# Ten dense matmuls of the mixing tables ahead of the first strided unit of batch 0

## The chip, the cores and the metric

The kernel runs on one core of one Trainium2 chip. The metric is device time in microseconds (us) of one execution, as the median of several runs. TensorE (PE) multiplies, VectorE (DVE) and ScalarE (ACT) work on rows of data, GpSimd (POOL) and SyncE (SP) here mostly issue DMA transfers. Each engine takes its instructions in one fixed order.

## The reference, cut to what matters

Inputs are q, k, v of 4 batches, 8 heads, 576 tokens and head size 64, then two mixing networks with weights of 512 x 2048 and 2048 x 512 each.

```
mask_local   = (rel >= 0) & (rel < 32)                       # heads 0 to 3
mask_strided = (rel >= 0) & (pos[None, :] % 32 == pos[:, None] % 32)   # heads 4 to 7
attn = softmax(where(mask, q @ k.T / 8, -1e9));  x = attn @ v          # per batch and head
x = x laid out as (batch, 576, 512)
h = x.transpose(0, 2, 1) @ U @ V;  u = x + h.transpose(0, 2, 1)
x = u + relu(u @ w_ch1) @ w_ch2                              # first network
u = x + real(fft2(x));  un = layer_norm(u)
out = u + relu(un @ w2_ch1) @ w2_ch2                         # second network
```

## The kernel before, in words

The attention of a batch is cut into nine units, taken in the order `L00, L10, L01, L11, R, S00, S10, S01, S11`: four local ones, one for the rest rows, and four strided ones (`strided_unit`), S*ji* for head pair *j* and half *i* of the token groups. A strided unit has three steps. First the mask is written into a PSUM bank by one matmul (L472) and the scores are added to it by five or six matmuls (L477). The maximum of each row is taken (L412) and negated (L415) on DVE, and ACT makes six exponentials (L420). Then three transposes on PE (L484) and two copies on ACT (L494, L491). Last the product with v, six matmuls (L500), and on DVE a reciprocal and a multiply (L425, L426, L432 in `norm_out`) that leave the unit's result in the tile `xs`. Banks of PSUM come from `bank()` in a fixed rotation.

When the four strided units of a batch are done, `unpermute` writes `xs` to DRAM (L554, L555 on SP's queue) and reads it back in the order of the tokens (L559, L561). Meanwhile `mix_groups` multiplies the rows with the table `US` (L577), and `VS` turns that back into 512 columns (L617), which L618 adds to the rows that `unpermute` has brought. `US` and `VS` are the mixing tables U and V, spread over 128 rows at the start; both are in the format f32r. Then `prep_tile` scales and splits the rows (L660, L143 to L147, L155, L158), transposes them on PE (L647), and the first layer of network 1 begins (L978 to L980), then its second (L1005 to L1007).

Beside this the lane of the weights runs: 512 KB pieces come by DMA into three buffers (`raw`, L162) and are turned from f64 bits into f32 (L135 to L139), squared for their scale (L213) and split in two f16 parts (L155, L158), on the same ACT and DVE. `wnow[0]` holds from the start until the second row tile of network 1 is prepared: batch 0's attention lies within it.

The code is written out as lanes that are stepped in a fixed sequence, and a scheduler then settles for each engine, when the kernel is built, in which order its instructions stand. A change in one place can so change the order of other instructions around it.

Of the kernel before, what the change touches and what calls it, by code (L numbers as in the profile page):

```python
# [35 lines left out]
RWIN = [256, 289]  # L36
MAGIC = 0x5F3759DF
RAWS = 3
BSEQ = [0, 1, 0, 1, 2]
PB = 1  # L40
LOADS = ['l0', 'm', 'v1', 'r', 'v0', 'l1', 'w', 's0', 'w', 'x0', 'w', 's1', 'x1']
# [30 lines left out]
def fused_kernel(ctx: ExitStack, tc: tile.TileContext, ql, kl, vl, vr, qs, ks, vs, uraw, vraw,  # L72
                 w11, w12, w21, w22, cb, cf, ft, out):
    nc = tc.nc
    V, A, T, G, S = nc.vector, nc.scalar, nc.tensor, nc.gpsimd, nc.sync

    const = ctx.enter_context(tc.tile_pool(name="const", bufs=1))
    wp = ctx.enter_context(tc.tile_pool(name="wp", bufs=1))
    rawp = ctx.enter_context(tc.tile_pool(name="rawp", bufs=RAWS))
    tmp = ctx.enter_context(tc.tile_pool(name="tmp", bufs=2))  # L80
# [8 lines left out]
    wnow = [True]  # L89

    def bank():
        if wnow[0]:
            nbk[0] += 1
            z = BSEQ[nbk[0] % len(BSEQ)]
            if z:
                return (pf1, pf2)[z - 1].tile([128, 512], F32, tag=f"f{z}", name="bk")
        return pb.tile([128, 512], F32, tag="b", name="bk")
# [69 lines left out]
    def fetch():  # L167
        if todo:
            src, m = todo.pop(0)
            pre.append((src, m, wload(src, m)))  # L170
# [106 lines left out]
    US = cst.tile([128, 12, 128], F32R, name="US")  # L277
    VS = cst.tile([128, 960], F32R, name="VS")
# [22 lines left out]
    def p_buf():  # L301
        if wnow[0]:
            return early_buf("gh", 416)
        return atp.tile([128, 416], F32, tag="P", bufs=PB, name="P")
# [103 lines left out]
    def softmax_rows(P, Sb, r, groups):  # L408
        mx = atp.tile([128, 8], F32, tag="mx", bufs=3, name="mx")
        c = 0  # L410
        for o, n, w in groups:
            V.tensor_reduce(out=mx[r, c:c + n], in_=Sb[r, o:o + n * w].rearrange("p (n w) -> p n w", n=n),  # L412
                            axis=AX.X, op=ALU.max)
            c += n
        V.tensor_scalar(out=mx[r, 0:c], in0=mx[r, 0:c], scalar1=-0.125, scalar2=None, op0=ALU.mult)  # L415
        c = 0
        for o, n, w in groups:
            for i in range(n):
                a = o + i * w
                A.activation(out=P[r, a:a + w], in_=Sb[r, a:a + w], func=AF.Exp,  # L420
                             scale=0.125, bias=mx[r, c:c + 1])
                c += 1
# [5 lines left out]
    def norm_out(O, dst, r, n):  # L428
        Ov = O[r, 0:130 * n].rearrange("p (n h w) -> p n h w", h=2, w=65)
        rc = atp.tile([128, 3, 2, 1], F32, tag="rc", bufs=3, name="rc")  # L430
        recip(rc[r, 0:n], Ov[:, :, :, 64:65])
        V.tensor_tensor(out=dst.rearrange("p n (h w) -> p n h w", h=2), in0=Ov[:, :, :, 0:64],  # L432
                        in1=rc[r, 0:n].to_broadcast([r.stop - r.start, n, 2, 64]), op=ALU.mult)
# [34 lines left out]

    def strided_unit(b, j, u, q, k, v, xs):
        Sb = bank()  # L470
        msk = mS[u].rearrange("p (n w) -> p n w", n=1).to_broadcast([128, 3, 128]) if u else mS[u]
        T.matmul(Sb[:, 0:384], lhsT=idb, rhs=msk, start=True, stop=True)  # L472
        for i in range(6):
            g = 6 * u + i - (u or i > 0)
            if u == 0 and i == 1:
                continue
            T.matmul(Sb[SROW, 64 * i:64 * i + 54], lhsT=q[:, 108 * g:108 * g + 108], rhs=k[:, 54 * g:54 * g + 54],  # L477
                     start=False, stop=True, skip_group_check=True)
        P = p_buf()
        softmax_rows(P, Sb, SROW, [(0, 6, 64)])  # L480
        yield
        Tb = bank()
        for t in range(3):
            T.transpose(Tb[:, 108 * t:108 * t + 108], P[SROW, 128 * t:128 * t + 128], ident[SROW, SROW])  # L484
        npz[0] += 1
        PT = early["pz"] if wnow[0] and npz[0] % 2 else PZ
        for e in range(2):
            r = slice(64 * e, 64 * e + 64)
            src = Tb[r, 0:324].rearrange("p (n c) -> p n c", c=54)
            if e:  # L490
                A.activation(out=PT[r, :, 27:81], in_=src, func=AF.Copy)  # L491
            else:
                dst = PT[r].rearrange("p n (f c) -> p n f c", c=27)[:, :, 0:4:3, :]
                A.activation(out=dst, in_=src.rearrange("p n (f c) -> p n f c", c=27), func=AF.Copy)  # L494
        yield
        O = bank()
        for t in range(3):
            for h in range(2):
                c = 65 * (2 * t + h)
                T.matmul(O[SROW, c:c + 65], lhsT=PT[:, 2 * t + h, :], rhs=v[:, 3 * u + t, h, :],  # L500
                         start=True, stop=True, skip_group_check=True)
        norm_out(O, xs[SROW, 3 * u:3 * u + 3, 128 * j:128 * j + 128], SROW, 3)
        yield
# [29 lines left out]
    def attn_units(b):  # L533
        xs = atp.tile([128, NT, 256], F32, tag="xs", bufs=1, name="xs")
        qk_upto(4 * b + 3)
        v = loaded if b == 0 else {n: VT[n[0]](b, int(n[1:] or 0)) for n in ("v0", "v1", "r", "x0", "x1")}
        for u in ORDER:
            if u == "R":
                yield u, rest_unit(b, qk[4 * b:4 * b + 2], v["r"]), xs
                qk_upto(4 * b + (5 if b else 4))  # L540
                continue
            j, i = int(u[1]), int(u[2])
            if u[0] == "L":
                yield u, local_unit(b, j, i, *qk[4 * b + j], v[f"v{j}"]), xs
            else:
                yield u, strided_unit(b, j, i, *qk[4 * b + 2 + j], v[f"x{j}"], xs), xs
                if i == 1 and b:
                    qk_upto(4 * b + 6 + j)
# [478 lines left out]
    def weights():  # L1027
# [6 lines left out]
        todo.extend((w, i) for w in (w21, w22) for i in range(NW))  # L1034
        for _ in range(RAWS):
            fetch()
# [279 lines left out]
```

## Time and the profile before

| | us |
|---|---|
| median of 3 runs | 967.18 (966.31 to 968.62) |
| profiled execution, its own time | 960.7 |
| its span, first to last instruction | 958.9 |
| PE busy | 910.7 (95% of the span) |
| DVE busy | 595.8 (62%) |
| ACT busy | 393.3 (41%) |
| mean granted clock of PE | 0.98 of full speed |

The profile tells of one execution. Its own time is 1.8 us more than its span and 6.5 us less than the median of the three runs; times in the rows are counted from the start of the span. Full speed of PE's clock is 2.4 GHz and its other level 1.2 GHz, shown as 1.00 and 0.50.

### The profile page before, as it was taken

Reading aid. Unit: us, or ns where it says so; the run is one execution under the profiler, and the core shown is the slowest. Engines: PE = TensorE matmul, PEld = TensorE weight load, DVE = VectorE, ACT = ScalarE, POOL = GpSimd, SP = SyncE. Lnnn points to the kernel's source line nnn. Section 1 sums busy time; section 2 is a strip of 40 time slices with the busy share of each in tenths; the row PEclk is TensorE's granted clock in tenths of the full one; section 3 lists DMA queues with packets and bytes.
Section 4 is the critical chain, followed back from the end, with each engine's and each line's share of the span. In section 5 each row is a group of like instructions: output and inputs, shape, how many; then the busy total and the mean of one; then the engine's idle time right before and its main releaser. Section 6 shows DMA issues by size and latency. Waiting matters only on the chain. (4 is left out here: it accounts for less than half of the span.)

```text
span 958.9 us, 14895 instructions
## 1 busy us (share of the span) xinstructions
PE 910.7 (95%) x5696; PEld 541.8 (57%) x5696; DVE 595.8 (62%) x1526; ACT 393.3 (41%) x947; POOL 48.9 (5%) x81
## 2 busy tenths in 40 slices
PE   5858999999999999999999989999999999999998
PEld 4737754555545664466456436555544657576565
DVE  3788888833342446862879998982799853142323
ACT  4867677624141434631447454241333333032122
POOL 0111011000000001100101300010000000000000
PEclk9859999999999999999999989999999999999999
DMA  9576675232211103601334520002022310200000
GB/s 298 166 260 196 204 263 163 67 117 96 65 23 23 39 3 118 155 22 34 100 94 127 127 72 1 1 19 70 1 55 50 94 23 1 61 2 1 23 23 23
DMA packets 68791, 78.58 MB, mean 82 GB/s; under 512 B 46384, under 2 KB 51760, under 8 KB 68720
## 3 DMA queue, kind: packets, MB, share of 16 engines
q1 hardware_dynamic: 59696, 44.49, 16.7%
q0 software_dynamic: 9024, 33.14, 10.9%
q8 instruction: 45, 0.74, 0.3%
q14 instruction: 26, 0.21, 0.1%
HBM read 60.18 MB, written 7.08 MB: 70 GB/s over the span
## 5 line engine op out<-in xcount | busy, mean ns | idle before, releaser
L1005 PE MATMUL f<-wslot,gh 128*128 128x512 f16 x576 | 218.1, 379 | 2.3 <-DVE ub L1013 1.9
L1006 PE MATMUL f<-wslot,gh 128*128 128x512 f16 x576 | 218.1, 379 | 0.1
L1007 PE MATMUL f<-wslot,gl 128*128 128x512 f16 x576 | 218.1, 379 | 0.0
L978 PE MATMUL f<-ut,wslot 128*128 128x512 f16 (+1 forms) x480 | 170.3, 355 | 9.9 <-DVE gl L985 9.2
L979 PE MATMUL f<-ut,wslot 128*128 128x512 f16 (+1 forms) x480 | 169.8, 354 | 1.1 <-DMA ut<-lo 1.1
L980 PE MATMUL f<-ut,wslot 128*128 128x512 f16 (+1 forms) x480 | 169.6, 353 | 0.0
L1013 DVE SCALAR_TENSOR_TENSOR ub<-f,ivt,ub 128x512 f32<-128x512 f32 x64 | 47.7, 746 | 113.2 <-PE f L1007 113.0
L984 ACT ACTIVATE gh<-f 128x512 f16<-128x512 f32 (+1 forms) x120 | 64.0, 535 | 120.2 <-PE f L980 119.7
L985 DVE SCALAR_TENSOR_TENSOR gl<-f,gh 128x512 f16<-128x512 f32 (+1 forms) x120 | 73.8, 615 | 55.1 <-ACT gh L984 54.3
L1007 PEld LDWEIGHTS <-gl 128*128 128x128 f16 x576 | 56.4, 98 | 66.9 <-issue 0.3
L1006 PEld LDWEIGHTS <-gh 128*128 128x128 f16 x576 | 56.7, 98 | 63.9 <-issue 2.8
L1005 PEld LDWEIGHTS <-gh 128*128 128x128 f16 x576 | 57.0, 99 | 63.0 <-issue 0.2
L979 PEld LDWEIGHTS <-wslot 128*128 128x128 f16 x480 | 47.4, 99 | 52.7 <-issue 15.4
L978 PEld LDWEIGHTS <-wslot 128*128 128x128 f16 x480 | 47.6, 99 | 43.8 <-issue 4.7
L980 PEld LDWEIGHTS <-wslot 128*128 128x128 f16 x480 | 47.3, 99 | 43.2 <-issue 1.6
L155 ACT ACTIVATE wslot<-wslot,wsc 128x512 f16<-128x512 f32 x64 | 46.0, 719 | 32.5 <-DVE wslot L158 22.2
L135 ACT ACTIVATE wslot<-raw 128x512 f32<-128x512 f32 x64 | 42.8, 675 | 38.5 <-DMA raw<-in_w 27.5
L906 ACT ACTIVATE wslot<-X 128x512 f32<-128x512 f32 (+1 forms) x24 | 12.6, 524 | 101.6 <-PE X L901 101.6
L158 DVE SCALAR_TENSOR_TENSOR wslot<-wslot,wsc 128x512 f16<-128x512 f32 x64 | 48.6, 759 | 5.4 <-ACT wslot L155 5.3
L162 POOL DMA_DIRECT2D raw<-in_w x61 | 33.4, 547 | 310.0 <-DVE fa L707 61.8
L213 ACT ACTIVATE wslot<-wslot 128x512 bf16<-128x512 f32 x64 | 40.3, 630 | 18.8 <-DVE wslot L139 16.3
L420 ACT ACTIVATE P<-bk,mx 108x64 f32<-108x64 f32 (+2 forms) x126 | 31.3, 329 | 39.2 <-DVE mx L415 35.9
(305 smaller groups left out, 1462.9 us busy)
## 6 DMA issues: line engine op xcount, KB each, us to landing
raw<-in_w POOLq DMA_DIRECT2D x61, 512.0 KB, 4.0
q<-in_ql SPq DMA_DIRECT2D x8, 576.0 KB
q<-in_qs SPq DMA_DIRECT2D x7, 594.0 KB
out<-ub SPq DMA_DIRECT2D x16, 256.0 KB
vl<-in_vl SPq DMA_DIRECT2D x8, 390.0 KB
vs<-in_vs SPq DMA_DIRECT2D x8, 390.0 KB
k<-in_kl SPq DMA_DIRECT2D x8, 320.0 KB
scr<-xs SPq DMA_DIRECT2D x8, 270.0 KB
```

The lines of the kernel that those rows point to most:

```text
L135: A.activation(out=dst, in_=hi.bitcast(F32), func=AF.Copy, scale=2.0 ** -112)
L155: A.activation(out=dst, in_=src, func=AF.Copy, scale=s)
L158: V.scalar_tensor_tensor(out=dst, in0=src, scalar=s, in1=hi, op0=ALU.mult, op1=ALU.subtract)
L978: T.matmul(ps[:, 0:n], lhsT=wh, rhs=uh[:, k, cols], start=(k == 0), stop=False)
L979: T.matmul(ps[:, 0:n], lhsT=wh, rhs=ul[:, k, cols], start=False, stop=False)
L980: T.matmul(ps[:, 0:n], lhsT=wl, rhs=uh[:, k, cols], start=False, stop=(k == 3))
L984: A.activation(out=gh[:, i, cols], in_=ps[:, 0:n], func=AF.Relu)
L985: V.scalar_tensor_tensor(out=gl[:, i, cols], in0=ps[:, 0:n], scalar=0.0, in1=gh[:, i, cols], op0=ALU.max, op1=ALU.subtract)
L1005: T.matmul(ps, lhsT=ga, rhs=w[:, 0, :], start=(i == 0), stop=False)
L1006: T.matmul(ps, lhsT=ga, rhs=w[:, 1, :], start=False, stop=False)
L1007: T.matmul(ps, lhsT=gb, rhs=w[:, 0, :], start=False, stop=(i == HW - 1))
L1013: V.scalar_tensor_tensor(out=utile(t), in0=ps, scalar=iv, in1=utile(t), op0=ALU.mult, op1=ALU.add)
```

## The change

When batch 0's first strided unit (S00) is recorded, ten matmuls are put ahead of its mask matmul. Each multiplies 128 columns of `US` with 512 columns of `VS` and writes the whole bank that S00 has just got. Their result is not used: the mask matmul that follows writes the bank anew.

```
+BURST = 10
...
     def strided_unit(b, j, u, q, k, v, xs):
         Sb = bank()
+        if wnow[0] and u == j == 0:
+            for _ in range(BURST):
+                T.matmul(Sb, lhsT=US[:, 0, :], rhs=VS[:, 0:512], start=True, stop=True,
+                         skip_group_check=True)
         msk = mS[u].rearrange("p (n w) -> p n w", n=1).to_broadcast([128, 3, 128]) if u else mS[u]
         T.matmul(Sb[:, 0:384], lhsT=idb, rhs=msk, start=True, stop=True)
```

Lines behind the insertion move down by five, those between by one: the mask matmul L472 becomes L477, the scores L477 become L482, the transposes L484 become L489, the product L500 becomes L505, and L577 becomes L582. The burst itself is L474.

Three places of the fixed orders differ. On PE, at the first strided unit, the order of before is this (L511 are the scores of the rest unit, L461 the product of the last local one, L517 and L527 the rest unit's transpose and product; `bk` is a bank, `cbt` holds masks and an identity, `gh` and `gl` hold exponentials and their transposes):

```order
L511 MATMUL bk<-k,q 64x64 x4
L472 LDWEIGHTS cbt
L472 MATMUL bk<-cbt 128x384
L477 MATMUL bk<-k,q 108x54 x5
L461 MATMUL bk<-vl,gl 64x65 x8
L517 MATMUL bk<-ident,gh 128x128
L472 LDWEIGHTS cbt
L472 MATMUL bk<-cbt 128x384
L527 MATMUL bk<-vr,gl 32x65 x8
```

At the same place the changed kernel has:

```order
L516 MATMUL bk<-k,q 64x64 x4
L474 MATMUL bk<-VS,US 128x512 x4
L462 MATMUL bk<-vl,gl 64x65 x8
L474 MATMUL bk<-VS,US 128x512 x2
L522 MATMUL bk<-ident,gh 128x128
L474 MATMUL bk<-VS,US 128x512 x4
L477 LDWEIGHTS cbt
L477 MATMUL bk<-cbt 128x384
L482 MATMUL bk<-k,q 108x54 x5
L532 MATMUL bk<-vr,gl 32x65 x8
```

The scores of S00 now stand behind the ten matmuls and also behind the local unit's product and the rest unit's transpose, which stood behind them before.

On DVE, at the third strided unit (S01), the order of before is this (the first row takes S01's maxima and the third negates them, the fifth and the seventh do so for S11; the last row is L425, the first step of a unit's normalization, here of S10; L137 to L139 and L136 belong to the lane of the weights):

```order
L412 TENSOR_REDUCE mx<-bk 108x6
L432 TENSOR_TENSOR xs<-bk,rc 108x3x128
L415 TENSOR_SCALAR mx<-mx 108x6
L137 SCALAR_TENSOR_TENSOR wslot<-wslot,raw 128x512
L412 TENSOR_REDUCE mx<-bk 108x6
L139 SCALAR_TENSOR_TENSOR wslot<-raw,wslot 128x512
L415 TENSOR_SCALAR mx<-mx 108x6
L136 TENSOR_SCALAR raw<-raw 128x512
L425 TENSOR_SCALAR rc<-bk 108x6
```

In the changed kernel it is (the first row takes S01's maxima, the second begins S10's normalization, the third negates S01's maxima):

```order
L413 TENSOR_REDUCE mx<-bk 108x6
L426 TENSOR_SCALAR rc<-bk 108x6
L416 TENSOR_SCALAR mx<-mx 108x6
L413 TENSOR_REDUCE mx<-bk 108x6
L427 RECIPROCAL rc<-rc 108x6
L140 SCALAR_TENSOR_TENSOR wslot<-raw,wslot 128x512
L433 TENSOR_TENSOR xs<-bk,rc 108x3x128
L416 TENSOR_SCALAR mx<-mx 108x6
```

The negation of S01's maxima now stands behind the first step of S10's normalization; before, both S01's and S11's were done ahead of it.

On PE, at the product of the last strided unit (S11, which uses `PZ`), the order of before is this (`ut` are the split rows that L577 multiplies with `US`):

```order
L577 MATMUL bk<-ut_515,US 128x256
L577 MATMUL bk<-ut_516,US 128x256
L500 MATMUL bk<-vs,PZ 108x65 x6
L577 MATMUL bk<-ut_515,US 128x256
L577 MATMUL bk<-ut_516,US 128x256
```

In the changed kernel it is:

```order
L505 MATMUL bk<-vs,PZ 108x65 x4
L582 MATMUL bk<-ut_526,US 128x256
L582 MATMUL bk<-ut_525,US 128x256
L582 MATMUL bk<-ut_526,US 128x256
L505 MATMUL bk<-vs,PZ 108x65 x2
```

Three mixing matmuls now stand between the fourth and the fifth of the six matmuls of that product. POOL and SP keep their orders.

## Rows read from the trace of the kernel before

**Rows 1.** Windows of stages: stretch, its length, busy us (instructions) by engine, PEclk, DMA.

```profile
41.40:48.30 6.90, 6.90 (x36) 6.78 (x36) 5.25 (x12) 5.68 (x16) 0.53 (x1) 0.50 0.38 127
...
71.30:180.00 108.70, 100.70 (x738) 66.30 (x736) 93.36 (x228) 80.68 (x202) 11.65 (x22) 1.00 0.62 194
```

**Rows 2.** Windows where the granted clock (PEclk, third from the end) changes.

```profile
40.00:40.50 0.50, 0.33 (x4) 0.13 (x2) 0.42 (x2) 0.50 (x3) 0.00 (x0) 1.00 0.59 66
40.50:41.00 0.50, 0.00 (x0) 0.00 (x0) 0.50 (x3) 0.49 (x2) 0.00 (x0) 0.55 1.03 221
...
71.00:72.00 1.00, 1.00 (x10) 0.81 (x9) 0.85 (x4) 0.59 (x2) 0.00 (x0) 0.86 1.02 410
```

**Rows 3.** PE timeline: start us, us, line, out<-in, form, xcount [idle <-releaser]; last local units.

```profile
16.62 1.16 PE L461 MATMUL bk<-vl,gl 96*64 96x65 f32 x16 [0.49 <-ACT VS L341]
...
24.10 0.73 PE L461 MATMUL bk<-vl,gl 96*64 96x65 f32 x16
```

**Rows 4.** PE timeline, from S00's mask matmul to S10's product.

```profile
27.49 0.34 PE L472 MATMUL bk<-cbt 128*128 128x384 bf16 x1
...
28.66 0.75 PE L461 MATMUL bk<-vl,gl 96*64 96x65 f32 x16
29.33 0.33 PE L517 MATMUL bk<-ident,gh 128*128 128x128 f32 x1
29.50 0.33 PE L472 MATMUL bk<-cbt 128*128 128x384 bf16 x1
...
32.71 1.32 PE L500 MATMUL bk<-vs,gh 128*108 128x65 f32 x12 [0.19 <-issue]
33.87 0.33 PE L472 MATMUL bk<-cbt 128*128 128x384 bf16 x1
...
35.29 0.88 PE L477 MATMUL bk<-ub 128*108 128x54 f32 x8
...
38.70 1.35 PE L500 MATMUL bk<-vs,PZ 128*108 128x65 f32 x12 [0.98 <-ACT PZ L491]
```

**Rows 5.** ACT timeline: the exponentials (L420) of S00, S10 and S01.

```profile
29.88 1.36 ACT L420 ACTIVATE gh<-bk,mx 108x64 f32<-108x64 f32 x6
...
35.32 0.66 ACT L135 ACTIVATE wslot<-raw 128x512 f32<-128x512 f32 x1 [1.40 <-DMA raw<-in_w]
36.01 1.55 ACT L420 ACTIVATE gh<-bk,mx 108x64 f32<-108x64 f32 x7
...
38.67 1.14 ACT L420 ACTIVATE gh<-bk,mx 108x64 f32<-108x64 f32 x5
```

**Rows 6.** DVE timeline: negated maxima of S01, S10's normalization, the last of S11's.

```profile
36.27 0.16 DVE L415 TENSOR_SCALAR mx<-mx 108x6 f32<-108x6 f32 x1
...
40.08 0.16 DVE L425 TENSOR_SCALAR rc<-bk 108x6 f32<-108x6 f32 x1 [1.25 <-PE bk L500]
...
49.71 0.55 DVE L432 TENSOR_TENSOR xs<-bk,rc 108x384 f32<-108x384 f32 x1
```

**Rows 7.** Timelines of SP, DVE and PE: from `xs` to the first network.

```profile
50.28 0.71 SPq L555 DMA_DIRECT2D scr<-xs  x2
55.46 1.25 SPq L559 DMA_DIRECT2D ub<-scr  x2
...
60.17 0.69 DVE L618 TENSOR_TENSOR ub<-ub,bk 128x512 f32<-128x512 f32 x1 [0.73 <-DMA ub<-scr]
...
68.72 0.42 PE L978 MATMUL f<-ut,wslot 128*128 128x256 f16 x1
```

**Rows 8.** PE timeline: matmuls of 512 columns in a row, at half and at full clock.

```profile
564.59 0.63 PE L980 MATMUL f<-ut,wslot 128*128 128x512 f16 x1
565.01 0.63 PE L978 MATMUL f<-ut,wslot 128*128 128x512 f16 x1
...
570.75 0.38 PE L979 MATMUL f<-ut,wslot 128*128 128x512 f16 x1
570.96 0.38 PE L980 MATMUL f<-ut,wslot 128*128 128x512 f16 x1
```

## The prediction

> **What bounds the kernel now.** I read the windows by stage first. From 71.3 us on PE is the bound: in 71.3 to 180 it is busy for 100.70 of 108.70 us [rows 1], so whatever moves the first matmul of network 1 moves the end. The stage ahead of that matmul is bounded by a chain, which the timelines show when followed back from it. Network 1 begins at 68.72, 8.55 us after L618 could add the first rows; that add waited until 60.17 for the rows read back from DRAM; the reading was issued at 55.46 and needs the writing of 50.28; and the writing needs the last strided unit's normalization, L432 at 49.71 [rows 7]. So the four strided units of batch 0 are the path, and each us by which the last of them is late is late at 68.72 too, as nothing behind 50.28 on that path waits for PE's matmuls alone.
>
> The next thing to read is PE's clock. The window rows show 1.00, then 0.55 in 40.5 to 41.0, 0.50 until 71, and 0.86 in 71 to 72 [rows 1, 2]. Of the first 23 us the column has no record; there the matmuls tell it: the same 16 of L461 take 1.16 us at 16.62 and 0.73 us at 24.10 [rows 3], so PE ran at half speed at first, and at full speed when the strided units began at 27.49. The fall at 40.5 follows pauses of PE (one of 0.98 us ends at 38.70 [rows 4]; in 40.5 to 41.0 it does nothing [rows 2]).
>
> **The price of the burst.** The trace has no ten f32r matmuls of 512 columns in a row. The nearest rows are those of 512 f16 columns: starts 0.43 us apart at half clock, 0.21 us at full clock [rows 8]. I take full clock, which rules at 27.49: 10 x 0.215 = 2.15 us. At half clock it would be 4.3 us, the upper bound of this term. Below, the burst could cost nothing if PE had that much free time ahead of the path; but S00's mask matmul starts at 27.49 without a wait before it [rows 4].
>
> **What is moved.** The new order puts two more things ahead of S00's scores: the local unit's product and the rest unit's transpose. They take PE from 28.66 to 29.50 [rows 4], 0.84 us, and stood behind S00's scores before. S00's mask matmul thus starts at 27.49 + 2.15 + 0.84 = 30.48, 3.0 us late.
>
> **What is carried on.** From S00's mask matmul to its product took 5.22 us (27.49 to 32.71), and S01's mask matmul stands behind that product, 1.16 us on (33.87) [rows 4]. Taken over, and with two transposes of S10 now ahead of it (0.2 us together), S01 starts at 30.48 + 5.22 + 1.16 + 0.2 = 37.06, 3.2 us late. S10's product now stands behind four scores of S11: 1.42 us from S01's mask to the first of these and 0.8 us for the four (33.87, 35.29 [rows 4]), so it starts at 39.3 in place of 38.70. Its end releases L425, 1.38 us after its start (38.70 to 40.08 [rows 4, 6]): 40.7. And here the new DVE order bites: S01's maxima are negated behind this L425, at 40.8, where they were ready at 36.27 [rows 6]. S01's six exponentials, 1.36 us like S00's, then end at 42.3; they ended at 38.67 + 1.14 = 39.81 before [rows 5]. That is 2.5 us late. S10's own exponentials gain: they stood behind a conversion that waited 1.40 us for a DMA at 35.32 [rows 5] and no longer do, but S10 is not the last unit.
>
> From there on S01 and S11 go as before, except at S11's product: three mixing matmuls of 256 columns, 3 x 0.21 = 0.64 us at half clock [rows 8], stand before its last two matmuls. Some wait themselves for rows that ACT and DVE split late. Walking all rows of the new orders of PE, ACT, DVE, POOL and SP in this way, each with its duration from the trace, started when its inputs and the row ahead of it are done, and the clock's levels at the times of before, the last L432 is 4.1 us late and network 1 starts 4.0 us late. (The same walk of the orders of before puts that start at 67.7, where the trace has 68.72, so its error is about 1 us in the whole and less in a difference.)
>
> **What is given back.** Before, network 1 spends its first 2.6 us at half clock: 68.72 to 71.3, as 0.86 in 71 to 72 means that 0.28 of that us was at 0.50 [rows 2, 7]. Starting 4 us later, it would find full clock if the rise comes at the same time: at most 1.3 us back. The walk gives 0.4 us, as PE waits there for DVE and ACT too; if the rise waits for network 1's own matmuls, it is nothing. The 8.0 us that PE idles in 71.3 to 180 [rows 1] could take in some delay if the weights came at fixed times; but the weights' lane uses the same ACT and DVE queues, which wait for the same matmuls, and in the walk nothing more is taken in. I take 4.0 - 0.5 = 3.5 us.
>
> The profiled execution's own time, 960.7, so becomes 964.2. The median of the runs shown is 967.18, 6.5 above that execution, and I carry the difference over: 967.18 + 3.5 = 970.7 us. Two tenths of a per cent, 1.9 us, is about what can be told from no change here.
>
> **A rule that speaks for the change.** The clock fell in before while PE paused. That would be worth avoiding: PE has 6.90 us of work without a pause at half clock from 41.4 to 48.3 [rows 1]. The Trainium skill, "TensorE: Matmul & The Clock Gate", section "What's actually happening", says that the lower clock is the default and that activity of the engine releases it; by that rule ten dense matmuls would help the clock, and the sum would be the 967.6 of the first rival below instead of 970.7. The rows agree in part only: 6.90 us of unbroken work in 41.4 to 48.3 did not raise it [rows 1].
>
> **The rivals.**
> The clock holds. If the burst kept full clock until about 64, the walk gives network 1 a start 1.0 us later than before, and 0.4 us behind the first 40 us of it: 967.6, no change. For it: S01's and S11's work would run at twice the speed. Against it: the burst ends some 10 us ahead of the pauses at which the clock fell, and right behind it the walk finds new ones: PE waits for S00's exponentials with 2.2 us idle between 33.2 and 35.6.
>
> The clock falls sooner, in that new hole, at about 37: the walk gives 6.6 us, 973.8. If a run has half clock all through, the burst costs 4.3 us itself and the walk gives +5.9, 973.1.
>
> It ends faster: the burst raises the clock. The runs shown are 6.5 us above the profiled execution. If that is because their PE never left half clock in the first 71 us (the walk of before gives +8.6 for that), and the burst's 4.3 us of dense work lifts it at 31, the walk of the changed kernel is 2.5 us shorter than that of before if the clock then falls at 44, and 5.5 us if it holds to 64: 961.7 to 964.7. This decides from the point where S00's and S10's scores run at full clock in the changed kernel and did not in those runs. The unbroken work that did not raise the clock [rows 1] speaks against it.
>
> The delay is hidden: ACT's wait of 1.40 us for a DMA [rows 5] and the pauses of PE (0.98 us at 38.70 [rows 4]) take in most of it, 0 to 1.6 us are left, 967.2 to 968.8.
>
> **How the numbers follow.** The delay as worked out: 0.50, in its own range 969.4 to 972. The clock falls sooner or is low throughout: 0.13. The clock holds: 0.14. Hidden: 0.10. The burst raises the clock: 0.13. Faster is the last one alone, 0.13; within 0.2% are the clock that holds and the hidden delay, 0.24; slower is the rest, 0.63. The range reaches from 965.0, into the raised clock, to 974.0, the sooner fall and the burst at half clock.
>
> **What would show it.** In the changed profile ten L474 rows of 0.21 to 0.22 us start to start from about 27.5; S00's mask matmul (now L477) near 30.5; the second negation of a 108x6 tile ending a wait for PE near 41; the last L433 near 54 and the first L983 near 72 to 73, at half clock before and between. Wrong: L474 rows 0.43 us apart; PEclk at 1.00 through 41 to 57; L983 near 69.

## The result and the profile after

The changed kernel takes 967.85 us (median of 20 runs, 961.69 to 977.35). Before, run beside it, takes 960.99 (20 runs, 953.36 to 970.12). The ratio is 1.0061, interval 1.0037 to 1.0085: the change costs 5.9 us, 3.6 to 8.2. (The ratio is of the runs as a whole: the means of all 20 give 1.0062, while the medians, which jump when runs fall into two groups, lie 6.9 us apart.) The predicted 970.7 us (965.0 to 974.0) holds the time, but the predicted delay of 3.5 us is just under that interval: of before's 20 runs 11 took 953.4 to 961.3 and 9 took 965.1 to 970.1, and the three runs that the prediction was built on, which are among the 20, were all of the second group. A second comparison (below) gave 5.2 us, 1.6 to 8.8, in which 3.5 lies.

The new order is also wider than the three places named ahead: ahead of 55 us the order of ACT differs too (the conversion that waited for a DMA [rows 5] now stands behind S10's exponentials), and DVE's does from S00 on. Behind 55 us PE, DVE and ACT have the order of before.

The profiled execution of after is the slowest of its 20 (977.35 us, span 975.6); its amounts are those of a bad case, its steps are read for what follows what. First PE's timeline at the strided units, which answers to [rows 4] (start us, us, line, out<-in, form, count, [idle <-releaser]):

```profile
28.98 2.08 PE L474 MATMUL bk<-VS,US 128*128 128x512 f32 x4
30.99 1.07 PE L462 MATMUL bk<-vl,gl 96*64 96x65 f32 x16
31.99 0.73 PE L474 MATMUL bk<-VS,US 128*128 128x512 f32 x2
32.55 0.27 PE L522 MATMUL bk<-ident,gh 128*128 128x128 f32 x1
32.58 1.17 PE L474 MATMUL bk<-VS,US 128*128 128x512 f32 x4
33.59 0.34 PE L477 MATMUL bk<-cbt 128*128 128x384 bf16 x1
...
36.67 0.79 PE L489 MATMUL bk<-ident,gh 108*128 108x108 f32 x3
38.57 2.37 PE L505 MATMUL bk<-vs,gh 128*108 128x65 f32 x12 [1.11 <-issue]
...
45.27 2.38 PE L505 MATMUL bk<-vs,PZ 128*108 128x65 f32 x12
...
55.89 1.70 PE L505 MATMUL bk<-vs,PZ 128*108 128x65 f32 x8 [0.53 <-ACT PZ L496]
57.35 0.99 PE L582 MATMUL bk<-ut,US 108*128 108x256 f32 x3
58.13 0.85 PE L505 MATMUL bk<-vs,PZ 128*108 128x65 f32 x4
...
78.48 0.93 PE L983 MATMUL f<-ut,wslot 128*128 128x256 f16 x2
```

The first four matmuls of the burst take 2.08 us, the last four 1.17: PE was at half clock when the burst began, and rose during it. S00's mask matmul starts at 33.59 where it started at 27.49. S00's product then takes 2.37 us in place of 1.32: the clock is down again. The windows show that (as [rows 1]: stretch, length, busy us by engine, PEclk third from the end):

```profile
31.80:38.60 6.80, 5.60 (x57) 4.57 (x53) 5.77 (x20) 4.25 (x15) 1.06 (x2) 1.00 0.33 88
38.60:82.90 44.30, 32.87 (x147) 26.49 (x148) 29.23 (x71) 28.39 (x79) 4.19 (x7) 0.50 0.57 179
...
160.00:175.00 15.00, 13.33 (x50) 6.43 (x48) 11.04 (x20) 9.70 (x23) 1.59 (x3) 0.77 0.37 110
```

Full clock for 6.8 us, then 0.50 until network 1 has run for 4.4 us. A further dip in 160 to 175, 0.77, adds to this execution; before had 1.00 there. On DVE, and then SP, which answer to [rows 6, 7]:

```profile
47.69 0.17 DVE L426 TENSOR_SCALAR rc<-bk 108x6 f32<-108x6 f32 x1 [3.29 <-PE bk L505]
47.77 0.16 DVE L416 TENSOR_SCALAR mx<-mx 108x6 f32<-108x6 f32 x1
...
60.37 0.55 DVE L433 TENSOR_TENSOR xs<-bk,rc 108x384 f32<-108x384 f32 x1
...
60.95 0.71 SPq L560 DMA_DIRECT2D scr<-xs  x2
66.27 1.24 SPq L564 DMA_DIRECT2D ub<-scr  x2
```

S10's normalization (L426) waits 3.29 us for PE, and S01's negation (L416) follows right behind it, as forecast, though at 47.77 and not near 41. The last normalization is 10.7 us later than before's and network 1 9.8 us later; the way from the one to the other takes 18.1 us, 0.9 less than before. So of the 16.7 us between the spans of the two profiles (975.6 and 958.9) 9.8 are lost ahead of network 1. The other 6.9 are lost behind its start, where the order is that of before; the dip above is part of them.

### The profile page after: what moved, and what is told of

Its sections match the earlier page's. It is cut to its first block, busy times and chain, and to the rows that moved or that the text cites. A ratio compares the mean times of both kernels' runs of the same rounds, so it can differ in the third digit from the quotient of the medians.

```text
span 975.6 us, 14913 instructions
## 1 busy us (share of the span) xinstructions
PE 925.5 (95%) x5706; PEld 552.7 (57%) x5706; DVE 596.5 (61%) x1526; ACT 393.0 (40%) x947; POOL 48.8 (5%) x81
## 5 line engine op out<-in xcount | busy, mean ns | idle before, releaser
L1011 PEld LDWEIGHTS <-gh 128*128 128x128 f16 x576 | 56.7, 98 | 64.2 <-issue 3.1
L156 ACT ACTIVATE wslot<-wslot,wsc 128x512 f16<-128x512 f32 x64 | 46.0, 718 | 32.3 <-DVE wslot L159 22.1
L136 ACT ACTIVATE wslot<-raw 128x512 f32<-128x512 f32 x64 | 42.6, 671 | 38.6 <-DMA raw<-in_w 27.0
L421 ACT ACTIVATE P<-bk,mx 108x64 f32<-108x64 f32 (+2 forms) x126 | 31.2, 329 | 39.2 <-DVE mx L416 35.9
```

The costliest lines, as they stand in the source:

```text
L136: A.activation(out=dst, in_=hi.bitcast(F32), func=AF.Copy, scale=2.0 ** -112)
L156: A.activation(out=dst, in_=src, func=AF.Copy, scale=s)
L1011: T.matmul(ps, lhsT=ga, rhs=w[:, 1, :], start=False, stop=False)
```

## The experiments

The kernels were run beside before in three batches, 12 runs of each and 35 of before in each batch, the medians of before being 966.74, 967.17 and 966.21. "Order of before" means that ordering edges were given to the scheduler: an edge between two instructions of one engine says which stands first, and adds no wait. In an expectation, "the walk" is the replay of rows that the prediction describes.

**The burst with little work.**

```
-            T.matmul(Sb, lhsT=US[:, 0, :], rhs=VS[:, 0:512], ...)
+            T.matmul(Sb[:, 0:32], lhsT=US[:, 0, :], rhs=VS[:, 0:32], ...)
```

> Each of the ten matmuls writes 32 columns in place of 512; all else as in the changed kernel. This leaves nearly no time of PE to the burst (ten times about 0.1 us) and cannot raise the clock, but the scheduler still reorders the instructions behind it. Time theory (the burst's 2.2 us on PE are the cost): 0.3 to 1 us above before. Order theory (the new order of PE and DVE around S00, S10 and S01 is the cost): 2 to 3 us above before, with the last L433 2 to 3 us late at equal clock.

Measured: 972.60 us (968.18 to 977.43), ratio 1.0072 (1.0045 to 1.0100). In its profile the ten take 1.29 us:

```profile
27.09 1.29 PE L474 MATMUL bk<-VS,US 128*128 128x32 f32 x10
28.23 0.34 PE L477 MATMUL bk<-cbt 128*128 128x384 bf16 x1
```

With a sixteenth of the columns the kernel is as slow, so the PE time of 512 columns is not the whole of it. That left the new order and the clock. But the order here is a third one, neither that of before nor that of the changed kernel: S00's scores stand behind the local unit's product and ahead of the rest unit's transpose. In this profile PE was at full clock when the burst began (0.11 us from start to start), waits 0.75 us ahead of S00's product, and the clock falls during that product, at 35.7.

**A burst at the start.** On before, and then on the changed kernel:

```
+    for _ in range(18):
+        T.matmul(wzb[:, 0:512], lhsT=wz[:, 0:128], rhs=wz[:, 0:512], ...)   # a tile of ones
```

> The kernel before with 18 bf16 matmuls of 512 columns on a tile of ones at the very start, where PE waits until 9.5 us for the first loads; the order of all other instructions is that of before. Clock theory (runs differ by how much of the first 70 us PE spends at half clock, and the burst's use is to raise it): full clock from about 6 us, network 1 at 66 to 68 us, median 956 to 958 and a narrower spread than before. Delay theory (only the place in PE's queue matters): as before, within 1 us.

> The changed kernel with the same 18 matmuls at the very start. Delay theory: at full clock in both, 1 to 2 us above the kernel with the start matmuls alone. If the cost of the change were the clock alone, the two would be equal.

Measured: on before 968.82 us (961.01 to 972.04), ratio 1.0035 (0.9999 to 1.0071); on the changed kernel 971.29 (963.37 to 977.24), 1.0065 (1.0026 to 1.0104). In the first one's profile (961.02 us, one of its two fastest runs) PE runs the 18 at 1.46 to 7.1 and its clock rises, then PE waits 1.61 us for q, and the 16 matmuls of a local unit take 1.16 us again at 16.24: this rise is lost before the strided units begin, and an early burst alone gains nothing.

**Nine in place of ten**, `BURST = 9`, with the same order as ten.

> Nine matmuls in place of ten: the same order as the changed kernel on every engine. Time theory: 0.2 us (full clock) to 0.4 us (half clock) below the changed kernel, so 4 to 7 us above before. A second look at the same order, for the clock: if the burst raises it in each run, the clock is at half until the burst's last matmuls, full at S00's scores, and half again by 45.

Measured: 971.68 us (964.37 to 973.69), 1.0063 (1.0029 to 1.0097): one matmul less changes nothing that can be told. In its profile S00's product waits as in after, and runs at half clock:

```profile
36.67 2.40 PE L505 MATMUL bk<-vs,gh 128*108 128x65 f32 x12 [1.10 <-issue]
```

**Burst and order apart.** Two kernels complete a square with before and after: the burst in the order of before, and the order of after without the burst.

```
+EDGES = [(316, 347), (358, 382), (383, 378), ...]      # 30 pairs; 18 others for the order of after
+        for a, b in EDGES:
+            tc.add_manual_dep(nc.get_inst_by_name(f"I-{a}"), f"I-{b}",
+                              mybir.DependencyInfo(mybir.DependencyClass.NoSync, ...), reason="order")
```

> The ten 512-column matmuls stand ahead of S00's mask matmul, but every other instruction of each engine stands in the order of before (30 ordering edges hold it there; nothing else differs). Theory A (the new order costs, the burst itself next to nothing): as before, within 1 us, network 1 starts within 1 us of where the same clock would have it in before. Theory B (the burst's own PE time costs, the new order nothing): as the changed kernel, 0.5 to 0.7% above before. Walking all rows in this order gives network 1 a start 3.3 us later than before under the clock of before's profile and 4.6 us later under the clock of the changed kernel's profile: 0.35 to 0.5% slower. In the profile: S10's product directly behind S01's and S11's negated maxima, as in before.

> No burst, but every instruction of each engine stands in the order of the changed kernel (18 ordering edges). Theory A (order): as slow as the changed kernel or nearly, 0.3 to 0.6% above before. Theory B (burst's own time): as before, within 0.2%. The walk gives network 1 a start 3.5 us later than before under the clock of before's profile, 3.2 us later under that of the changed kernel's: 0.3 to 0.4% slower. In the profile: S01's negated maxima end a wait for S10's product, three mixing matmuls stand within S11's product.

Measured: the burst in the order of before 964.68 us (960.39 to 968.27), ratio 0.9986 (0.9958 to 1.0014), **not slower**; the new order without the burst 969.33 (962.25 to 974.32), 1.0028 (1.0000 to 1.0057). As differences, the burst alone gives -1.3 us (-4.1 to 1.4), the order alone 2.7 (0 to 5.5), both 5.9 (3.6 to 8.2). By itself the burst costs at most 1.4 us; the walk had it at 3.3, so it failed there. What happens instead shows in the burst's profile in the order of before:

```profile
28.08 3.60 PE L475 MATMUL bk<-VS,US 128*128 128x512 f32 x10
31.52 0.34 PE L478 MATMUL bk<-cbt 128*128 128x384 bf16 x1
31.69 1.07 PE L483 MATMUL bk<-k,q 128*108 128x54 f32 x10
32.69 0.75 PE L463 MATMUL bk<-vl,gl 96*64 96x65 f32 x16
33.37 0.33 PE L523 MATMUL bk<-ident,gh 128*128 128x128 f32 x1
...
36.75 1.32 PE L506 MATMUL bk<-vs,gh 128*108 128x65 f32 x12 [0.19 <-issue]
...
72.99 0.42 PE L984 MATMUL f<-ut,wslot 128*128 128x256 f16 x1
```

Here too the burst starts at half clock (3.44 us to the mask; ten at 0.215 would be 2.15) and ends at full. But S00's scores stand ahead of the local product (L463) and the rest transpose (L523), and these give PE work while DVE and ACT turn S00's scores into exponentials. PE waits 0.19 us ahead of S00's product; in after it waits 1.11 us, as that work has gone ahead. The windows from S00's mask to its product, of the burst in the order of before and then of after:

```profile
31.52:36.75 5.23, 4.62 (x60) 3.92 (x59) 3.83 (x14) 2.98 (x12) 0.53 (x1) 1.00 0.15 20
```

```profile
33.59:38.57 4.98, 3.78 (x42) 3.31 (x42) 4.25 (x15) 3.49 (x14) 0.89 (x2) 1.00 0.44 118
```

PE is without work for 0.61 us of the one stretch and 1.20 us of the other. Where the clock falls: at 44.0 in the order of before, some 13.6 us after the rise (the burst's matmuls start 0.41 to 0.43 us apart up to 30.36 and 0.22 to 0.23 from there, so it rose near 30.4), at 38.6 in after, where PE's pause at S00 ends. For the first:

```profile
43.50:44.00 0.50, 0.50 (x8) 0.50 (x7) 0.00 (x0) 0.50 (x3) 0.00 (x0) 0.98 0.00 0
44.00:44.50 0.50, 0.47 (x4) 0.13 (x1) 0.45 (x2) 0.37 (x2) 0.00 (x0) 0.50 0.47 66
```

**One edge: S01's negation back in its place.** On the changed kernel, `EDGES = [(456, 441)]`.

> The changed kernel with one ordering edge: S01's maxima are negated ahead of the first step of S10's normalization on DVE, as in before; burst and PE's order at S00 stay. If the place of that negation is what costs (the prediction: S01's exponentials 2.5 us late because of it), this returns to within 0.2% of before. If it is only one of several things in the order, the walk gives back 0.7 to 0.9 us: 0.5% above before, not to be told from the changed kernel. In the profile: the negation of S01's maxima no longer ends a wait for S10's product.

Measured: 970.49 us (965.30 to 975.82), ratio 1.0055 (1.0023 to 1.0087). The negation no longer waits for S10's product:

```profile
42.31 0.17 DVE L417 TENSOR_SCALAR mx<-mx 108x6 f32<-108x6 f32 x1
42.97 0.17 DVE L427 TENSOR_SCALAR rc<-bk 108x6 f32<-108x6 f32 x1 [0.49 <-PE bk L506]
```

and the time is that of the changed kernel. (Behind S01's maxima the edge moved a few other rows too: some of the weights' lane on DVE and ACT, and one of S11's transposes on PE.) The 0.7 to 0.9 us that the walk gave to this edge can't be told by time. The profiles say more: in this one the clock, though PE's order and pause at S00 are those of after, holds to 47.9, and in that of the changed kernel with the start burst, whose order is that of after on every engine, it holds to 47.0. S00's mask, its product and S01's product there:

```profile
32.41 0.34 PE L477 MATMUL bk<-cbt 128*128 128x384 bf16 x1
...
37.39 1.32 PE L505 MATMUL bk<-vs,gh 128*108 128x65 f32 x12 [1.10 <-issue]
...
45.53 1.35 PE L505 MATMUL bk<-vs,gh 128*108 128x65 f32 x12 [1.20 <-ACT gh L496]
```

and with the edge:

```profile
33.10 0.34 PE L478 MATMUL bk<-cbt 128*128 128x384 bf16 x1
...
38.08 1.32 PE L506 MATMUL bk<-vs,gh 128*108 128x65 f32 x12 [1.10 <-issue]
...
46.28 1.35 PE L506 MATMUL bk<-vs,gh 128*108 128x65 f32 x12 [0.46 <-ACT gh L497]
```

At this equal clock S01's product starts 13.12 us behind S00's mask with the late negation and 13.18 with the early one: the swap on DVE delays nothing there. And the pause does not bring the clock down in each execution.

**Filling PE's pauses.** Matmuls of 512 columns on a tile of ones, result unused, in the order of before: 18 at the start, one to eight in each pause, 30 ahead of the last wait.

> Before's order on each engine, and 115 matmuls of 512 bf16 columns on a tile of ones (result unused) in the pauses of PE: 18 while q is awaited at the start, 1 to 8 in each pause up to S11's product and in the mixing, 30 in the wait ahead of the row transposes of network 1. Theory C (what separates the executions of before near 957 from those near 968 is whether PE's clock rises ahead of the strided units, and it falls in PE's pauses): the clock rises at about 5 to 8 us and holds; network 1 starts at 65 to 66 us at full clock; 955 to 958 us, 1% below before, with little spread. Rival (clock is not held by filling pauses, or fills at half clock stand in the way): network 1 starts at 73 to 91 us, 972 to 990.

Measured: 967.79 us (962.95 to 970.40), 1.0011 (0.9984 to 1.0038): no gain, and the profile shows two faults of this kernel:

```profile
19.63 0.42 PE L442 MATMUL bk<-cbt 128*128 128x416 bf16 x1 [2.40 <-DVE ub L433]
...
70.82 8.19 PE L1116 MATMUL wzb<-wz 128*128 128x512 bf16 x29 [0.24 <-issue]
78.85 0.61 PE L648 MATMUL bk<-idh,gl 128*128 128x128 f16 x8
```

The fills held a bank of their own, and a local unit waited 2.40 us for one that had been free before; and 29 of the last 30 stood behind the wait that they were to fill, 8.2 us on the path. The fills did hold the clock: it is full from 23.2 to 64.2.

**The last four, side by side.** The changed kernel again; five wide matmuls in the order of before (`BURST = 5`, 23 edges); ten narrow ones in the order of before (21 edges); and a mended fill, whose fills are written into the bank that the next step gets:

```
+FILL = {1: 8, 3: 6, 8: 4, 4: 3, 7: 1, 6: 1, 10: 1, 9: 1, 15: 2, 17: 1, 19: 1, 22: 4, 27: 4, 29: 1, 32: 12}
...
+            t = (pb, pf1, pf2)[z].tile([128, 512], F32, tag=f"f{z}" if z else "b", name="bk")
+            for _ in range(FILL.get(nbk[0] - 1, 0)):
+                T.matmul(t, lhsT=wz[:, 0:128], rhs=wz, start=True, stop=True, skip_group_check=True)
+            return t
...                                                     # and 25 such matmuls at the start
```

> The changed kernel once more, so that it stands beside the runs of before and of the kernels below on one chip. Theory A (the new order costs about 3 us, and keeps the clock that the burst raises from holding): 0.5 to 0.8% above before. Rival (the first comparison overstated it): 0.2 to 0.4%, the 3.5 us of the prediction.

> Five of the 512-column matmuls in place of ten, every other instruction in the order of before (23 edges). Theory A (in the order of before the burst raises the clock where it would not have risen, and costs its own time where it would have): between before and the ten in the same order, 962 to 967, if five still raise the clock in every execution; the walk gives network 1 a start 1.0 us later than before at full clock. Rival (five are too few): executions without an early rise are back, 966 to 970.

> Ten matmuls of 32 columns in place of 512 (1.3 us of PE in the earlier run of them with the new order), every other instruction in the order of before (21 edges). Theory A (the same ten narrow matmuls were 0.7% slower with the new order because of the order): within 0.2% of before; the walk gives 0.0 to 0.4 us. As they do not raise the clock, the spread stays that of before, with executions near 957 and near 968. Rival (anything ahead of S00 costs): 0.5% or more above before.

> Before's order, with 75 matmuls of 512 bf16 columns of ones, none behind S11's product but 12 ahead of the first row transposes: 25 while q is awaited, then 1 to 8 in each pause, written into the bank that the next step gets (the earlier filled kernel kept a bank of its own, which made a local unit wait 2.4 us at 19.6, and had 30 that ended up behind the transposes, 8.2 us on the path). Theory C (a clock that rises at 5 to 8 us and holds is worth 2 us against the executions of before near 957 and up to 10 against those near 968): network 1 starts at 65 to 67 us, 955 to 960 in nearly all executions. Rival (the fills come at half clock, or another pause lets the clock fall): a start at 70 to 77, 963 to 970.

| kernel | median us (range) | ratio (interval) |
|---|---|---|
| changed, again | 969.35 (965.29 to 976.62) | 1.0054 (1.0017 to 1.0091) |
| five wide, order of before | 965.85 (960.10 to 970.45) | 0.9997 (0.9970 to 1.0024) |
| ten narrow, order of before | 970.15 (961.79 to 973.17) | 1.0060 (1.0022 to 1.0098) |
| mended fill | 960.43 (957.52 to 965.73) | 0.9958 (0.9932 to 0.9985) |

The second profile of the changed kernel shows the same thing at S00 as the first: the wait, and behind it half clock (2.39 us for the product):

```profile
32.86 0.34 PE L477 MATMUL bk<-cbt 128*128 128x384 bf16 x1
...
37.84 2.39 PE L505 MATMUL bk<-vs,gh 128*108 128x65 f32 x12 [1.10 <-issue]
```

Five wide matmuls are not to be told from ten by time, and the clock rises during them too. They stand 1.93 us ahead of S00's mask, and the clock holds to 42.2; network 1 starts at 69.54.

The ten narrow matmuls are a miss of the order theory, which had them at no cost in the order of before. Their profile:

```profile
28.14 2.32 PE L475 MATMUL bk<-VS,US 128*128 128x32 f32 x10
30.30 0.50 PE L478 MATMUL bk<-cbt 128*128 128x384 bf16 x1
...
77.98 0.42 PE L984 MATMUL f<-ut,wslot 128*128 128x256 f16 x1
```

They take 0.22 us each at half clock, 2.16 us ahead of S00's mask, where the walk had a delay of 0.4 at most. And here they don't raise the clock: S00's scores (1.92 us for the ten rows that took 1.07 at full clock) and all behind them run at half until network 1, which starts at 77.98, 9.3 us after before's. So the narrow burst of the first batch does not show that the order costs, as had been read from it: it is as slow in the order of before. It loses by its own 1.3 to 2.3 us and, by the mean clocks told at the end, by executions whose clock rises late: 8 of 12 here and 6 of 12 in the first batch, against 22 of 105 of before.

The mended fill beats both kernels, by 4.1 us against before (1.4 to 6.6). In its profile:

```profile
5.00:18.00 13.00, 10.93 (x74) 6.31 (x73) 6.62 (x19) 5.73 (x17) 0.00 (x0) 1.00 1.03 290
...
25.50:52.00 26.50, 22.59 (x217) 17.50 (x217) 20.88 (x61) 23.15 (x69) 3.98 (x7) 1.00 0.44 136
52.50:62.00 9.50, 6.65 (x19) 4.06 (x19) 7.50 (x16) 5.81 (x13) 1.05 (x2) 0.50 0.76 249
```

Full clock from 5 to 18 and through all of the strided units, where before's profile, one of its better executions, had it from 23.5 to 40.5. Its network 1 starts at 68.46, like before's 68.72: the gain is not against such executions, but that more of them are now like them (8 of 12 below 962 us, where 12 of before's 35 were, and none above 965.7, where before went to 975.1). The expected 65 to 67 us were not reached; the clock first fell at 18.1, behind a wait of 2.07 us for a load, and the fills of that stretch came at half clock.

**The profiles side by side.** The way from S00's mask matmul to the last normalization, in the profiles of all kernels with one of the two orders and no fills, against the clock at that place:

| order | kernel | PE waits ahead of S00's product | full clock until | mask to last normalization |
|---|---|---|---|---|
| before | before | 0.19 us | 40.5 | 22.2 us |
| before | start burst | 0.18 | 39.2 | 22.2 |
| before | ten wide | 0.19 | 44.0 | 22.3 |
| before | five wide | 0.18 | 42.2 | 22.1 |
| before | ten narrow | none | at half clock | 28.8 |
| after | changed | 1.11 | 38.6 | 26.8 |
| after | changed, again | 1.10 | 37.8 | 26.8 |
| after | nine | 1.10 | 36.3 | 25.6 |
| after | changed, start burst | 1.10 | 47.0 | 20.9 |
| after, but for one edge | one edge | 1.10 | 47.9 | 20.2 |
| after | no burst | 1.09 | at half clock | 29.3 |

Where the clock holds over the wait at S00, the new order is no slower on this way than the old one; where it falls there, in three of the five profiles that came to S00's mask at full clock, 4.7 to 6.6 us are lost. (The two that held had full clock for 14.7 us behind the mask, the four of the old order for 12 to 13.) At half clock all through, the new order loses 0.5 us on this way (29.3 against 28.8) and 2.1 ahead of it. There the rest unit's scores and S00's mask start at, without the burst:

```profile
25.88 0.70 PE L512 MATMUL bk<-k,q 128*64 128x64 f32 x8
...
28.62 0.53 PE L473 MATMUL bk<-cbt 128*128 128x384 bf16 x1
```

That is 2.74 us from the one to the other; with the ten narrow ones it is 2.79, of which the burst takes 2.16 (the scores start at 27.51). The sum of the two losses, 2.6, is near the 2.7 that the order alone cost in time (from two executions, so no more than a hint).

## Why the prediction was right or wrong

**Right: what bounds the first stage.** Network 1 moved with the last normalization (60.37 and 78.48 against 49.71 and 68.72 [rows 6, 7]). That the end moves with network 1 alone does not hold in these profiles: both of the changed kernel take 6.5 to 6.9 us more than before's from network 1's start to the end, and that of the ten wide in the order of before, no slower by time, takes 3.0 more.

**Wrong: "I take full clock, which rules at 27.49".** In all seven profiles of a wide burst at S00 its first matmuls run at half clock (2.08 us for four in after). The full clock of [rows 3] belongs to one kind of execution; the three runs shown were, by their times, of the other, and the prediction carried the 6.5 us between them over and left what they were to one rival. The burst, with the 0.84 us of L461 and L517, so took 4.61 us to S00's mask (28.98 to 33.59), not the 2.99 of the sum.

**Wrong: that the burst's PE time is the loss.** In the order of before the same ten matmuls cost 3.44 us at S00 and nothing in the whole (0.9986), and the clock rises during them for the units behind. This is the mechanism of the rival that ends faster; that "the unbroken work that did not raise the clock speaks against it" was the wrong inference: in 6.90 us of f32 work the clock did not rise [rows 1], in the ten matmuls of 512 columns it did. The Trainium skill, "TensorE: Matmul & The Clock Gate", section "What's actually happening", has activity release the clock; the runs agree for the wide matmuls (3.44 us to the mask, 2.15 at full clock and 4.3 at half), while 6.90 us of small f32 ones in one place [rows 1] and the ten narrow ones in another passed without a rise; yet before's clock rose at 23.5 behind small f32 ones alone:

```profile
18.64 3.75 PE L445 MATMUL bk<-k,q 128*128 128x96 f32 x16 [0.39 <-DMA q<-in_ql]
22.18 1.11 PE L453 MATMUL bk<-ident,gh 128*96 128x128 f32 x4
23.62 0.33 PE L453 MATMUL bk<-ident,gh 128*128 128x128 f32 x1 [0.32 <-ACT gh L420]
```

**Right in kind, wrong in weight: the order.** The local unit's product and the rest unit's transpose ahead of S00's scores are the part of the order that I can point to: priced at 0.84 us of PE time, they also took away the work that filled PE's wait for S00's exponentials. That the clock could fall in such a hole was one rival, which shared a chance of 0.13 with another. The hole is 1.10 to 1.11 us in all five profiles with this order of PE and a wide burst, and in three of them the clock was down when S00's product ran behind it. That "the new DVE order bites" was wrong: at equal clock S01's product comes no later for it (13.12 us behind S00's mask, 13.18 with the negation put back).

**The smaller steps.** The three mixing matmuls within S11's product are there and take 0.78 us at half clock (57.35 to 58.13; 0.64 forecast). The way from the last normalization to network 1 is 0.9 us shorter in the profile of after, 0.1 forecast (4.1 and 4.0 us late). Of the 0.5 us that network 1 was to get back by starting later, nothing is seen: it runs at half clock for 4.4 us there, 2.6 before. Of the rivals, "the clock falls sooner, in that new hole, at about 37", at 6.6 us, is what both traces of after show (it fell at 38.6, and at 37.8 in the second), and 5.9 us is nearer to it than to 3.5. A clock that holds until 64 is seen in none; the longest hold with a burst at S00 is to 47.9.

**Right by chance: the total.** 3.5 us were made of a burst at full clock and a late negation; what the runs show behind the measured 5.9 (and 5.2) is the new order, 2.7 by itself, and a rise of the clock that three of five profiles lose at S00. The absolute 970.7 fits since its base was 6.2 us too high (967.18 against 960.99) and its delay, 6.9 us between the medians, 3.4 too small.

**Open.** The burst and the order together cost 4.5 us more than the sum of the two alone, but with intervals of 2 to 3 us on each of the three, from different batches, that is only about what they can tell. That the pause at S00 brings the clock down is likely, not shown: the clock fell there in three of five profiles with the same pause, and in none of the four with 0.2 us of pause that came there at full clock. What decides between the executions stays open, and with one execution of each kernel traced their share is not known. Why the changed kernel's profiles lose more behind network 1's start stays open too.

## What to carry to other kernels

Where a scheduler sets the order, test an inserted instruction in the old order as well: here the change in the order, which no line of the diff names, decided whether the burst cost anything. A single profile may show one of several kinds of execution; look first whether the spread of the times has two groups, and which one the profile is of. Dense matmuls without use can be worth their time: here 75 of them gained 4.1 us when they stood in PE's waits and wrote into the bank that was next in turn anyway, and 115 with a bank of their own, some on the path, gained nothing.

## What the runs showed of the hardware

A kernel whose instructions never change has executions near 957 and near 968 us. No trace of before's slower kind was taken, but that of the narrow burst in the order of before shows one where PE's clock first rises at about 82 (23.5 in before's). In the 22 us of it below PE was busy for 20.73, and its clock stayed at half, as the 2.32 us and the 1.92 us above show; the column PEclk reads 1.00 in such a stretch, since it has no record ahead of the first change, and only the spacing of equal matmuls tells the level:

```profile
28.00:50.00 22.00, 20.73 (x128) 18.91 (x126) 10.61 (x34) 11.12 (x37) 1.59 (x3) 1.00 0.22 69
```

So an execution whose clock rises late has a high mean granted clock: 0.994 in this one. That mean is on record for every run. Of the 105 runs of before in the three batches 22 have 0.99 or more, and none of them is below 965 us; the 26 below 962 us all lie between 0.975 and 0.983. Of the 80 runs of the six kernels that add five to ten wide matmuls at S00 and no others not one is above 0.982, so a late rise shows in none of them.

These f32r matmuls of 32 columns, ten in a row, start 0.11 us apart at full and 0.22 us at half clock, far more than a sixteenth of those of 512 (0.215 and 0.43).
